# V of each attention unit in one transfer, another order of early loads, and a second score buffer that also takes values

## The chip, the cores and the metric

The kernel runs on one core of a Trainium2 chip. The core has a matrix engine (TensorE: PE in the profile, and PEld for the loading of its stationary operand), VectorE (DVE), ScalarE (ACT), GpSimd (POOL), an engine that mostly issues transfers (SyncE, SP) and 16 DMA engines that they share. The metric is the device time of one execution in microseconds (us). Before the change three runs took 886.68, 889.40 and 889.49 us; the median is 889.40.

## The reference

Three stages follow one another, all in float32:

```python
# B=4, 8 heads, S=576, D=64; q, k, v: (4, 8, 576, 64)
scores = (q @ k.transpose(0, 1, 3, 2)) / 8
# heads 0..3: only the 32 latest positions; heads 4..7: only positions equal mod 32, not later
scores = where(mask, scores, -1e9); scores -= max(scores)
attn = exp(scores); attn /= sum(attn) + 1e-9
x = (attn @ v), heads side by side            # (2304, 512)
x = (sigmoid(x @ w_gate) * (x @ w_val)) @ w_out     # d_ff 1536
h = x @ w_in                                        # d_ff 2048
out = (max(h, 0) + log1p(exp(-abs(h)))) @ w_out2    # (2304, 512)
```

## The kernel before

**Precision.** A float32 matrix product is done as three products of high and low parts (`mm3`, lines 72 to 74). Activations are split on the chip (xh, xl). The weights come as packed 64-bit words in pieces of 128x512 (`raw`, 512 KB, line 109) and are decoded into their two parts by `decode_steps`: VectorE (lines 129, 133, 139, 146), ScalarE (157, the high part) and GpSimd (159 and 160, the low part).

**Attention.** It is cut into 16 units, one per batch and pair of heads; each batch has two local units (0, 1; 4, 5; ...) and two strided ones (2, 3; 6, 7; ...). A unit i passes through:

- `load(i)` and `load_v(i)`: transfers of Q (928), K (929) and V (947). V is stored in two halves of partitions, from 0 and from 64: for a local unit 64 partitions with 10 and 8 chunks of positions, for a strided one 54 partitions each, one transfer per half;
- `bias(i)` (1033) writes the mask into PSUM by a matmul, `scores(i)` (1052) adds QK in 48 or 80 small matmuls; VectorE takes the maximum (1070) and subtracts it (1071);
- `exponent(i)` on ScalarE (1078), `normalize(i)`: sums on VectorE (1085 to 1088), and the multiplication on GpSimd (1091);
- `p_transposes(i)`: six TensorE transposes (1114), copied out of PSUM by ScalarE (1118, later 1120);
- `values(i)` (1131): 72 matmuls for a local unit, 48 for a strided one, into a tile of `ps_o`;
- `outputs(i)`: ScalarE writes xh (1156), VectorE xl (1159).

After these come the gate and value products of the first gated layer, the second layer and the softplus layer; the first matmuls of the gates (lines 72 to 74, tile ps_g) are woven between the later units.

**Order.** Every engine executes its instructions in the order in which the program issues them; a framework adds the semaphore waits that the data and the buffers call for. For units 0 to 4 the order is written out by hand in `first()`; TURN is 4, the first unit of the second batch; from unit 5 on a function `stage(u)` takes over. Transfers of SP are issued in program order too, so a transfer that waits holds all behind it. `hold(t)` (line 100) puts a 1x1 GpSimd memset on a tile ahead of its load: the transfer then waits until GpSimd has come to that point. Eight semaphores (DMAHW0 to DMAHW7) go round among SP's transfers, so each also waits for the one that used its semaphore before.

**Buffers.** V has three buffers, and unit 3's V lies in a part of `acc[1]`; raw weights have three. In PSUM, in use at first are `ps_s` (scores), `ps_o` (values), and two pools that are closed at `early.close()`: `ps_s1` (the scores of units 1 and 3) and `ps_t` (transposes). What these two held is then given to `ps_hy` (three banks, which hold ps_g and its like) and `ps_x` (one bank).

Of the kernel before, what the change touches and what calls it, by code (L numbers as in the profile page):

```python
# [9 lines left out]
F32 = mybir.dt.float32  # L10
# [8 lines left out]
B, H, S, D = 4, 8, 576, 64  # L19
NT, DM = B * S, H * D  # L20
DFF, DFF2 = 1536, 2048
P = 128
STRIDE = 32
NPAIR = H // 2
NLP = NPAIR // 2
# [5 lines left out]
SQ = RG * NJ  # L31
HP = P // 2
HR = 2
NC = S // LQ
SLOTS_L = -(-NC // 4)
NL = (NC + 2) // 2, (NC - 2) // 2
RH = STRIDE // HR
NS = -(-RH // RG)
# [10 lines left out]
def tile_sparse_attention_moe_moe2(  # L49
# [10 lines left out]
    nc = tc.nc  # L60
# [812 lines left out]
    def attention():  # L873
        with ExitStack() as actx:
# [17 lines left out]
                "g": pool("gp", 1), "t": pool("tp", 2), "d": pool("decp", 1), "e": nc.gpsimd,  # L892
            }
            early = ExitStack()
            ps_s1, ps_t = (
                early.enter_context(tc.tile_pool(name=name, bufs=bufs, space=PSUM))
                for name, bufs in (("ps_s1", 1), ("ps_t", 2))
            )

            units = [(b, hp) for b in range(B) for hp in range(NPAIR)]  # L900
# [33 lines left out]
            def load_v(i, held=False):  # L934
                b, hp = units[i]
                loc, w, m, ns = dims(i)
                if i == NPAIR - 1:
                    t = acc[1][:, 0:NL[0] * 2 * D].rearrange("p (n h d) -> p n h d", h=2, d=D)
                else:
                    t = vp.tile([P, NL[0], 2, D], F32, tag="v", name="vt")  # L940
                src = vl[b, hp] if loc else vs[b, hp - NLP]
                if held:
                    hold(t[:, 0, 0, :])
                for r in range(HR):
                    n = NL[r] if loc else NS
                    o = r * HP
                    nc.sync.dma_start(out=t[o:o + w, 0:n], in_=src[r * w:(r + 1) * w, 0:n])
                vt[i] = t

            todo.extend((g, m, c) for g in range(2) for m in range(3) for c in range(GC))  # L950
# [6 lines left out]
            load_v(0)  # L957
            load(3)
            load_v(1)

            scratch = acc[NBA - 1]
            ident = scratch[:, 0:P]
# [160 lines left out]
            def values(i):  # L1123
                loc, w, m, ns = dims(i)
                pt, vv = pts.pop(i), vt.pop(i)
                ps = ps_o.tile([P, 2, TB], F32, tag="o", name="ps_o")
                for r, c, s, p0 in chunks(loc):
                    rows = slice(r * HP, r * HP + w)
                    o = s // 2 * P + p0
                    for h in range(2):  # L1130
                        nc.tensor.matmul(
                            ps[h * D:(h + 1) * D, r, c * m:(c + 1) * m],
                            lhsT=vv[rows, c, h, :], rhs=pt[rows, h, o:o + m],
                            start=True, stop=True,
                        )
                outs[i] = ps
# [51 lines left out]
            def first():  # L1188

                decs = [decode_steps(pools, refill) for refill in (False, False, True)]  # L1190
                swap = lambda: pools.update(f=[other])
                bias(0)
                scores(0)
                masks[False] = table("m_str", P + 2 * LK, SQ, SLOTS_S, strided)
                bias(1)
                scores(1)
                keep_busy(1)
                exponent(0)
                normalize(0)
                load_next(held=True)  # L1200
                load_next()
                bias(2)
                scores(2)
                exponent(1)
                normalize(1)
                load_v(2, held=True)
                load_v(3)
                keep_busy(1)
                bias(3)
                scores(3)  # L1210
                exponent(2)
                p_transposes(0)
                exponent(3)
                normalize(2)
                load(4, held=True)
                normalize(3)
                load_next(held=True)
                values(0)
                outputs(0)
                p_transposes(1)  # L1220
                p_transposes(2)
                next(decs[0])
                next(decs[0])
                load(5, held=True)
                values(1)
                outputs(1)
                p_transposes(3)
                swap()
                next(decs[1])
                next(decs[1])  # L1230
                load_next(held=True)
                load_v(4)
                values(2)
                outputs(2)
                bias(TURN)
                scores(TURN)
                early.close()
                pools["hy"] = pool("ps_hy", 3, space=PSUM)
                pools["x"] = pool("ps_x", 1, space=PSUM)
                values(TURN - 1)  # L1240
                outputs(TURN - 1)
                exponent(TURN)
                normalize(TURN)
                load(6, held=True)
                load_v(5)
                load_next()
                next(decs[2])
                yield
                next(decs[2])
                yield  # L1250
# [199 lines left out]
def _layout(inputs):  # L1450
# [25 lines left out]
        0, 1, 2, 4, 5, 3, 6  # L1476
    )
    z = z.reshape(B, NPAIR - NLP, 2, HR, NS, SQ, D).transpose(0, 1, 3, 5, 4, 2, 6)
    vs = np.ascontiguousarray(z).reshape(B, NPAIR - NLP, HR * SQ, NS, 2, D)

    def w_in(w):
        return w.reshape(NCC, P, -1, GC, P).transpose(2, 1, 3, 0, 4).reshape(-1, P, WE)
# [37 lines left out]
```

## Time and profile before

| what | us |
|---|---|
| median of three runs | 889.40 |
| lowest and highest run | 886.68, 889.49 |
| the profiled execution's own time | 887.71 |
| its span (first to last instruction) | 885.9 |
| PE busy in the span | 864.1 |

The profile is of one execution. Its mean granted TensorE clock is 0.994 of full speed. How the rows of the trace read:

- the page's first line gives, for each engine, busy us, share of the span, and instructions;
- a table of stretches has: start and end in us, length, then for PE, PEld, DVE, ACT and POOL the busy us and in brackets the number of instructions, the granted TensorE clock as a share of full speed, the busy share of the 16 DMA engines, and GB/s;
- a timeline of an engine has: start in us, length of the whole group in us, engine, line, operation, out<-in, shapes, the number of instructions, and in square brackets the idle time ahead of the group and what ended it ("issue": nothing that the profile shows). Matmuls overlap, so a group's length can reach into the next;
- the list of transfers gives: how many, KB of each, and the median us from issue to landing.

### The profile page before, as it was taken

Reading aid. Unit: us, or ns where it says so; the run is one execution under the profiler, and the core shown is the slowest. Engines: PE = TensorE matmul, PEld = TensorE weight load, DVE = VectorE, ACT = ScalarE, POOL = GpSimd, SP = SyncE. Lnnn points to the kernel's source line nnn. Section 1 sums busy time; section 2 is a strip of 40 time slices with the busy share of each in tenths; the row PEclk is TensorE's granted clock in tenths of the full one; section 3 lists DMA queues with packets and bytes.
Section 4 is the critical chain, followed back from the end, with each engine's and each line's share of the span. In section 5 each row is a group of like instructions: output and inputs, shape, how many; then the busy total and the mean of one; then the engine's idle time right before and its main releaser. Section 6 shows DMA issues by size and latency. Waiting matters only on the chain.

```text
span 885.9 us, 15388 instructions
## 1 busy us (share of the span) xinstructions
PE 864.1 (98%) x6008; PEld 725.1 (82%) x6008; DVE 600.3 (68%) x898; ACT 421.3 (48%) x680; POOL 490.7 (55%) x396
## 2 busy tenths in 40 slices
PE   7789999999999999999999999999999999999998
PEld 5668888888888888888888888888888878888887
DVE  5876876268878888878874645665756674656575
ACT  2456544423333333233333466666667575665641
POOL 5563321037888687688778625466536963343530
PEclk9899999999999999999999999999999999999999
DMA  7796450034675567566643245566665565545403
GB/s 245 191 260 165 125 156 9 1 99 139 237 257 195 190 242 243 182 214 225 227 166 158 76 148 176 191 198 197 198 231 187 189 220 184 186 149 181 152 1 118
DMA packets 61367, 153.01 MB, mean 173 GB/s; under 512 B 6160, under 2 KB 6672, under 8 KB 61296
## 3 DMA queue, kind: packets, MB, share of 16 engines
q1 hardware_dynamic: 61008, 151.42, 53.6%
q8 instruction: 47, 0.77, 0.4%
q10 hardware_dynamic: 288, 0.62, 0.2%
q14 instruction: 24, 0.20, 0.1%
HBM read 113.75 MB, written 38.27 MB: 172 GB/s over the span
## 4 chain that ended last, share of the span: by engine, by line
PE 72%; DVE 3%; ACT 1%; POOL 1%; issue 1%; DMA 0%; DVEq 0%; POOLq 0%; ACTq 0%; SPq 0%
PE ps_y L72 10%; PE ps_y L73 10%; PE ps_y L74 10%; PE ps_v L74 4%; PE ps_v L72 4%; PE ps_v L73 4%; PE ps_h L73 4%; PE ps_h L74 4%; PE ps_h L72 4%; PE ps_g L72 4%; PE ps_g L74 4%; PE ps_g L73 4%; PE ps_b L72 2%; PE ps_b L73 2%; PE ps_b L74 2%
## 5 line engine op out<-in xcount | busy, mean ns | idle before, releaser
L335 POOL TENSOR_TENSOR b<-b,b 128x512 f32<-128x512 f32 (+1 forms) x42 | 72.4, 1738 | 91.7 <-DVE gl L335 46.1
L248 ACT ACTIVATE gh<-ps_v 128x512 fp32r<-128x512 f32 (+1 forms) x60 | 33.3, 555 | 131.1 <-DVE ps_v L289 131.0
L309 DVE TENSOR_TENSOR acc<-ps_y,acc 128x512 f32<-128x512 f32 (+1 forms) x100 | 62.1, 633 | 48.0 <-PE ps_y L74 47.6
L338 ACT ACTIVATE gh<-b 128x1024 fp32r<-128x1024 f32 (+1 forms) x63 | 57.8, 917 | 40.6 <-DVE b L718 22.7
L474 DVE TENSOR_TENSOR acc<-ps_y,acc 128x512 f32<-128x512 f32 x66 | 44.8, 686 | 39.5 <-PE ps_y L74 38.4
L335 POOL TENSOR_TENSOR gl<-b,gh 128x1024 fp32r<-128x1024 f32 x20 | 49.1, 2457 | 36.5 <-ACT gh L338 36.5
L249 DVE TENSOR_TENSOR gl<-ps_v,gh 128x512 fp32r<-128x512 f32 (+1 forms) x60 | 38.3, 638 | 37.5 <-ACT gh L248 37.5
L196 POOL TENSOR_TENSOR a<-f,e 128x512 f32<-128x512 f32 x32 | 41.4, 1293 | 39.5 <-DVE e L146 39.5
L184 POOL TENSOR_TENSOR pair<-a,pair 128x512 fp32r<-128x512 f32 x32 | 41.5, 1296 | 31.9 <-ACT pair L183 31.9
L335 DVE TENSOR_TENSOR gl<-b,gh 128x1024 fp32r<-128x1024 f32 (+1 forms) x43 | 48.8, 1137 | 14.4 <-ACT gh L338 14.3
L72 PE MATMUL ps_y<-gh,w12h 128*128 128x512 f32 (+1 forms) x144 | 54.0, 375 | 0.1
L74 PE MATMUL ps_y<-gh,w02l 128*128 128x512 f32 (+1 forms) x144 | 53.7, 373 | 0.0
L73 PE MATMUL ps_y<-gl,w12h 128*128 128x512 f32 (+1 forms) x144 | 53.6, 373 | 0.0
L289 DVE TENSOR_TENSOR ps_v<-ps_v,sg 128x512 f32<-128x512 f32 (+1 forms) x60 | 38.5, 641 | 21.2 <-PE ps_v L74 20.0
L74 PE MATMUL ps_y<-gh,w12l 128*128 128x512 f32 (+1 forms) x140 | 52.2, 373 | 0.2 <-POOL w12l L160 0.2
L72 PE MATMUL ps_y<-gh,w02h 128*128 128x512 f32 (+1 forms) x136 | 51.3, 377 | 0.7 <-ACT acc L307 0.6
L183 ACT ACTIVATE pair<-s 128x512 fp32r<-128x512 f32 x32 | 20.2, 632 | 66.4 <-POOL s L210 51.8
L133 DVE SCALAR_TENSOR_TENSOR f<-raw,ps_x 128x512 uint32<-128x512 uint32 x66 | 45.4, 688 | 8.9 <-POOL w11l L160 2.1
L73 PE MATMUL ps_y<-gl,w02h 128*128 128x512 f32 (+1 forms) x136 | 50.6, 372 | 0.0
L146 DVE SCALAR_TENSOR_TENSOR e<-raw,ps_x 128x512 f32<-128x512 uint32 x66 | 45.3, 687 | 2.3
L139 DVE TENSOR_SCALAR ps_x<-f 128x512 uint32<-128x512 uint32 x66 | 45.4, 688 | 0.9
L72 PE MATMUL ps_g<-xh,w00h 128*128 128x512 f32 (+1 forms) x120 | 45.5, 379 | 0.0
(359 smaller groups left out, 2809.0 us busy)
## 6 DMA issues: line engine op xcount, KB each, us to landing
raw<-in_w_dram SPq DMA_DIRECT2D x68, 512.0 KB, 4.6
in_s<-pair SPq DMA_DIRECT2D x32, 512.0 KB, 3.4
out_s<-pair SPq DMA_DIRECT2D x32, 512.0 KB, 2.9
xh<-in_s SPq DMA_DIRECT2D x64, 256.0 KB, 3.3
xl<-in_s SPq DMA_DIRECT2D x56, 256.0 KB, 3.2
out_dram<-acc SPq DMA_DIRECT2D x16, 256.0 KB, 2.0
w10h<-out_s SPq DMA_DIRECT2D x6, 512.0 KB, 5.8
w10l<-out_s SPq DMA_DIRECT2D x6, 512.0 KB, 4.0
```

The source lines that it names most:

```text
L72: nc.tensor.matmul(ps, lhsT=lh, rhs=rh, start=first, stop=False, **kw)
L73: nc.tensor.matmul(ps, lhsT=lh, rhs=rl, start=False, stop=False, **kw)
L74: nc.tensor.matmul(ps, lhsT=ll, rhs=rh, start=False, stop=last, **kw)
L133: nc.vector.scalar_tensor_tensor(out=f, in0=high, scalar=0xC0000000, in1=part, op0=ALU.bitwise_and, op1=ALU.bitwise_or,)
L139: nc.vector.tensor_scalar(out=e, in0=f, scalar1=0xFF800000, scalar2=None, op0=ALU.bitwise_and)
L146: nc.vector.scalar_tensor_tensor(out=e.bitcast(F32), in0=low, scalar=2.0 ** -52, in1=x.bitcast(F32), op0=ALU.mult, op1=ALU.mult,)
L184: nc.gpsimd.tensor_tensor(out=l, in0=src, in1=h.bitcast(F32), op=ALU.subtract)
L196: nc.gpsimd.tensor_tensor(out=a, in0=f.bitcast(F32), in1=e.bitcast(F32), op=ALU.add)
L309: nc.vector.tensor_tensor(out=y, in0=ps[:, 0:n], in1=y, op=ALU.add)
L335: eng.tensor_tensor(out=out, in0=a, in1=b, op=ALU.subtract)
L338: nc.scalar.activation(out=op[0], in_=src, func=AF.Copy)
L474: nc.vector.tensor_tensor(out=y, in0=ps, in1=y, op=ALU.add)
```

## The change

Three things change. V comes to each unit in one transfer of 128 partitions: for the strided units the host pads the halves to 64 rows with zeros, and for the local ones the second half is loaded with all 10 chunks, of which `values` reads 8 as before. Second, the loads in `first()` are released in another order: two raw loads come ahead of the V of unit 2, unit 4's Q and K come earlier, unit 4's V waits for a memset behind the first decode, and the second step of decode 1 follows the outputs of unit 2. Third, values(1) and values(3) write to the pool `ps_s1` instead of `ps_o`; the order of the two closed pools is swapped, and values(3) and outputs(3) come ahead of `early.close()`.

```diff
--- before.py
+++ after.py
@@ -892,9 +892,9 @@
                 "g": pool("gp", 1), "t": pool("tp", 2), "d": pool("decp", 1), "e": nc.gpsimd,
             }
             early = ExitStack()
-            ps_s1, ps_t = (
+            ps_t, ps_s1 = (
                 early.enter_context(tc.tile_pool(name=name, bufs=bufs, space=PSUM))
-                for name, bufs in (("ps_s1", 1), ("ps_t", 2))
+                for name, bufs in (("ps_t", 2), ("ps_s1", 1))
             )
 
             units = [(b, hp) for b in range(B) for hp in range(NPAIR)]
@@ -938,13 +938,10 @@
                     t = acc[1][:, 0:NL[0] * 2 * D].rearrange("p (n h d) -> p n h d", h=2, d=D)
                 else:
                     t = vp.tile([P, NL[0], 2, D], F32, tag="v", name="vt")
-                src = vl[b, hp] if loc else vs[b, hp - NLP]
                 if held:
                     hold(t[:, 0, 0, :])
-                for r in range(HR):
-                    n = NL[r] if loc else NS
-                    o = r * HP
-                    nc.sync.dma_start(out=t[o:o + w, 0:n], in_=src[r * w:(r + 1) * w, 0:n])
+                n = NL[0] if loc else NS
+                nc.sync.dma_start(out=t[:, 0:n], in_=vl[b, hp] if loc else vs[b, hp - NLP])
                 vt[i] = t
 
             todo.extend((g, m, c) for g in range(2) for m in range(3) for c in range(GC))
@@ -957,6 +954,7 @@
             load_v(0)
             load(3)
             load_v(1)
+            load_next()
 
             scratch = acc[NBA - 1]
             ident = scratch[:, 0:P]
@@ -1123,7 +1121,10 @@
             def values(i):
                 loc, w, m, ns = dims(i)
                 pt, vv = pts.pop(i), vt.pop(i)
-                ps = ps_o.tile([P, 2, TB], F32, tag="o", name="ps_o")
+                if i < TURN and i % 2:
+                    ps = ps_s1.tile([P, 2, TB], F32, tag="s", name="ps_o")
+                else:
+                    ps = ps_o.tile([P, 2, TB], F32, tag="o", name="ps_o")
                 for r, c, s, p0 in chunks(loc):
                     rows = slice(r * HP, r * HP + w)
                     o = s // 2 * P + p0
@@ -1198,13 +1199,13 @@
                 exponent(0)
                 normalize(0)
                 load_next(held=True)
-                load_next()
+                load_v(2)
                 bias(2)
                 scores(2)
                 exponent(1)
                 normalize(1)
-                load_v(2, held=True)
-                load_v(3)
+                load_v(3, held=True)
+                load(4)
                 keep_busy(1)
                 bias(3)
                 scores(3)
@@ -1212,37 +1213,36 @@
                 p_transposes(0)
                 exponent(3)
                 normalize(2)
-                load(4, held=True)
+                load_next(held=True)
                 normalize(3)
-                load_next(held=True)
+                load(5, held=True)
                 values(0)
                 outputs(0)
                 p_transposes(1)
                 p_transposes(2)
                 next(decs[0])
                 next(decs[0])
-                load(5, held=True)
+                load_v(4, held=True)
+                load_next()
                 values(1)
                 outputs(1)
                 p_transposes(3)
                 swap()
                 next(decs[1])
-                next(decs[1])
-                load_next(held=True)
-                load_v(4)
                 values(2)
                 outputs(2)
+                next(decs[1])
+                load(6, held=True)
                 bias(TURN)
                 scores(TURN)
+                values(TURN - 1)
+                outputs(TURN - 1)
                 early.close()
                 pools["hy"] = pool("ps_hy", 3, space=PSUM)
                 pools["x"] = pool("ps_x", 1, space=PSUM)
-                values(TURN - 1)
-                outputs(TURN - 1)
                 exponent(TURN)
                 normalize(TURN)
-                load(6, held=True)
-                load_v(5)
+                load_v(5, held=True)
                 load_next()
                 next(decs[2])
                 yield
@@ -1476,7 +1476,9 @@
         0, 1, 2, 4, 5, 3, 6
     )
     z = z.reshape(B, NPAIR - NLP, 2, HR, NS, SQ, D).transpose(0, 1, 3, 5, 4, 2, 6)
-    vs = np.ascontiguousarray(z).reshape(B, NPAIR - NLP, HR * SQ, NS, 2, D)
+    vs = np.zeros((B, NPAIR - NLP, HR, HP, NS, 2, D), f)
+    vs[:, :, :, :SQ] = z
+    vs = vs.reshape(B, NPAIR - NLP, P, NS, 2, D)
 
     def w_in(w):
         return w.reshape(NCC, P, -1, GC, P).transpose(2, 1, 3, 0, 4).reshape(-1, P, WE)
```

**SyncE, the first transfers behind Q and K of units 0 to 2.** vt is unit 0's, then unit 1's, then unit 2's V; acc_64 is unit 3's V; the Q and K in between are unit 3's. Before:

```order
L947 DMA vt<-in_vl_dram 64x1280
L947 DMA vt<-in_vl_dram 64x1024
L928 DMA qt<-in_q_dram 128x622
L929 DMA kt<-in_k_dram 128x612
L947 DMA vt<-in_vl_dram 64x1280
L947 DMA vt<-in_vl_dram 64x1024
L109 DMA raw<-in_w_dram 128x512 x2
L947 DMA vt<-in_vs_dram 54x768 x2
L947 DMA acc_64<-in_vs_dram 54x768 x2
```

After:

```order
L944 DMA vt<-in_vl_dram 128x1280
L928 DMA qt<-in_q_dram 128x622
L929 DMA kt<-in_k_dram 128x612
L944 DMA vt<-in_vl_dram 128x1280
L109 DMA raw<-in_w_dram 128x512 x2
L944 DMA vt<-in_vs_dram 128x768
L944 DMA acc_64<-in_vs_dram 128x768
```

Each V has become one instruction; both raw loads still stand ahead of the V of unit 2.

**SyncE, the transfers behind Q and K of unit 4.** The raw loads are weights of decodes 2 and 3, Q and K are unit 5's, and vt is unit 4's V. Before, then after:

```order
L109 DMA raw<-in_w_dram 128x512 [waits DMAHW4_49,Pool_49]
L928 DMA qt<-in_q_dram 128x576 [waits DMAHW5_49,Pool_49]
L929 DMA kt<-in_k_dram 128x608 [waits DMAHW6_49]
L109 DMA raw<-in_w_dram 128x512 [waits DMAHW7_49,DVE_49,Pool_49]
L947 DMA vt<-in_vl_dram 64x1280 [waits DMAHW0_49,PE_49]
L947 DMA vt<-in_vl_dram 64x1024 [waits DMAHW1_49]
```

```order
L109 DMA raw<-in_w_dram 128x512 [waits DMAHW0_49,Pool_49]
L928 DMA qt<-in_q_dram 128x576 [waits DMAHW1_49,Pool_49]
L929 DMA kt<-in_k_dram 128x608 [waits DMAHW2_49]
L944 DMA vt<-in_vl_dram 128x1280 [waits DMAHW3_49,Pool_49]
L109 DMA raw<-in_w_dram 128x512 [waits DMAHW4_49,DVE_49]
```

Unit 4's V stood behind a raw load that waits for GpSimd and VectorE, and itself waited for PE; now it waits for GpSimd's memset and stands ahead of that raw load.

**TensorE, from values(2) to the first gates matmul (ps_g).** Between them stand bias(4), scores(4) and values(3), whose operands lie in acc_64. Before:

```order
L1131 MATMUL ps_o<-pt,vt 64x54 [waits DMAHW6_49,DVE_49,PE_49]
L1131 MATMUL ps_o<-pt,vt 64x54
L1131 MATMUL ps_o<-pt,vt 64x54 [waits DMAHW7_49]
L1131 MATMUL ps_o<-pt,vt 64x54 x21
L1033 MATMUL ps_s<-m_loc,one 128x320 x2
L1052 MATMUL ps_s<-kt,qt 32x64 [waits DMAHW3_49,DMAHW2_49]
L1052 MATMUL ps_s<-kt,qt 32x64 x39
L1131 MATMUL ps_o<-acc_64 64x54 [waits DMAHW0_49,DVE_49]
L1131 MATMUL ps_o<-acc_64 64x54 [waits Activation_49]
L1131 MATMUL ps_o<-acc_64 64x54 [waits DMAHW1_49]
L1131 MATMUL ps_o<-acc_64 64x54 x21
L72 MATMUL ps_g<-xh,w00h 128x512
L73 MATMUL ps_g<-xl,w00h 128x512
```

After:

```order
L1132 MATMUL ps_o<-pt,vt 64x54 [waits DMAHW4_49,DVE_49]
L1132 MATMUL ps_o<-pt,vt 64x54 x23
L1031 MATMUL ps_s<-m_loc,one 128x320 x2
L1050 MATMUL ps_s<-kt,qt 32x64 [waits DMAHW7_49,DMAHW6_49]
L1050 MATMUL ps_s<-kt,qt 32x64 x39
L1132 MATMUL ps_o<-acc_64 64x54 [waits DMAHW5_49,DVE_49,Activation_49]
L1132 MATMUL ps_o<-acc_64 64x54 [waits Activation_49]
L1132 MATMUL ps_o<-acc_64 64x54 x22
L72 MATMUL ps_g<-xh,w00h 128x512 [waits DVE_49]
L73 MATMUL ps_g<-xl,w00h 128x512
```

The first matmul of values(2) has lost a wait for PE, each V one semaphore, and the first gates matmul has a wait for VectorE that it did not have; by the program, that wait is for xl of outputs(3).

**VectorE, from xl of unit 1 to xl of unit 3.** acc_63 holds the working words of decode 1; ps_s are unit 4's scores; the rows with 128x2x18x16 are xl of units 2 and 3. Before:

```order
L1159 TENSOR_TENSOR xl<-ps_o,xh 128x320 [waits PE_49,Activation_49]
L1159 TENSOR_TENSOR xl<-ps_o,xh 128x256
L129 TENSOR_SCALAR acc_63<-raw 128x512 [waits DMAHW5_49]
L133 SCALAR_TENSOR_TENSOR acc_63<-raw,acc_63 128x512 [waits DVE_49]
L139 TENSOR_SCALAR acc_63<-acc_63 128x512 [waits DVE_49]
L146 SCALAR_TENSOR_TENSOR acc_63<-raw,acc_63 128x512 [waits DVE_49]
L1159 TENSOR_TENSOR xl<-ps_o,xh 128x2x18x16 [waits Activation_49]
L1070 TENSOR_REDUCE st<-ps_s 128x2x5 [waits PE_49]
L1071 TENSOR_TENSOR sl_109<-ps_s,st 128x640 [waits DVE_49]
L1159 TENSOR_TENSOR xl<-ps_o,xh 128x2x18x16 [waits Activation_49]
```

After:

```order
L1160 TENSOR_TENSOR xl<-ps_o,xh 128x320 [waits PE_49,Activation_49]
L1160 TENSOR_TENSOR xl<-ps_o,xh 128x256
L129 TENSOR_SCALAR acc_63<-raw 128x512 [waits DMAHW3_49]
L133 SCALAR_TENSOR_TENSOR acc_63<-raw,acc_63 128x512 [waits DVE_49]
L1160 TENSOR_TENSOR xl<-ps_o,xh 128x2x18x16 [waits Activation_49]
L139 TENSOR_SCALAR acc_63<-acc_63 128x512 [waits DVE_49]
L146 SCALAR_TENSOR_TENSOR acc_63<-raw,acc_63 128x512 [waits DVE_49,Pool_49]
L1068 TENSOR_REDUCE st<-ps_s 128x2x5 [waits PE_49]
L1069 TENSOR_TENSOR sl_109<-ps_s,st 128x640 [waits DVE_49]
L1160 TENSOR_TENSOR xl<-ps_o,xh 128x2x18x16 [waits Activation_49]
```

Unit 2's xl now stands between the two halves of decode 1; xl of unit 3 is still the last of the ten.

## Rows read from the trace of the kernel before

**Rows 1.** the page: busy us, share, instructions of each engine

```profile
PE 864.1 (98%) x6008; PEld 725.1 (82%) x6008; DVE 600.3 (68%) x898; ACT 421.3 (48%) x680; POOL 490.7 (55%) x396
```

**Rows 2.** table of stretches, the opening and 400 us of the steady part

```profile
0.00:50.00 50.00, 37.74 (x861) 29.49 (x861) 33.70 (x64) 17.21 (x32) 26.52 (x54) 0.90 0.79 225
100.00:500.00 400.00, 398.81 (x2525) 335.34 (x2524) 296.18 (x466) 140.26 (x243) 258.77 (x230) 1.00 0.50 168
```

**Rows 3.** timeline of PE from 12 to 66 us

```profile
15.01 1.54 PE L1052 MATMUL ps_s<-kt,qt 64*64 64x54 f32 x48 [2.15 <-DMA kt<-in_k_dram]
...
21.26 0.30 PE L1131 MATMUL ps_o<-pt,vt 64*64 64x32 f32 x3 [1.47 <-issue]
...
27.72 0.92 PE L1131 MATMUL ps_o<-pt,vt 54*64 54x54 f32 x48 [0.91 <-PE ps_p L1114]
...
31.33 0.93 PE L1131 MATMUL ps_o<-acc 54*64 54x54 f32 x48 [1.24 <-DVE xl L1159]
32.19 0.50 PE L72 MATMUL ps_g<-xh,w00h 128*128 128x512 f32 x1
...
35.96 0.44 PE L1114 MATMUL ps_p<-one,sl 128*128 128x128 f32 x2 [0.86 <-POOL sl L1091]
...
39.91 0.31 PE L1131 MATMUL ps_o<-pt,vt 64*64 64x32 f32 x4 [1.24 <-DMA vt<-in_vl_dram]
41.01 1.39 PE L1131 MATMUL ps_o<-pt,vt 64*64 64x32 f32 x68 [0.79 <-DMA vt<-in_vl_dram]
...
54.33 0.76 PE L1052 MATMUL ps_s<-kt,qt 64*64 64x54 f32 x35 [0.38 <-DMA kt<-in_k_dram]
...
63.69 0.54 PE L1052 MATMUL ps_s<-kt,qt 64*32 64x64 f32 x34 [1.89 <-issue]
```

**Rows 4.** table of stretches by the shape of the transfers in flight

```profile
3.00:6.80 3.80, 3.42 (x58) 2.18 (x58) 0.40 (x2) 0.00 (x0) 3.12 (x14) 1.00 1.05 402
7.50:10.00 2.50, 2.50 (x84) 2.00 (x84) 2.34 (x5) 0.71 (x1) 0.00 (x0) 1.00 1.00 220
19.00:22.00 3.00, 1.53 (x57) 1.39 (x50) 1.21 (x4) 0.54 (x3) 2.54 (x5) 0.92 0.57 179
```

**Rows 5.** timeline of SP's queue

```profile
7.95 0.43 SPq L929 DMA_DIRECT2D kt<-in_k_dram  x1
...
17.66 0.68 SPq L947 DMA_DIRECT2D acc<-in_vs_dram  x2
...
33.43 1.11 SPq L947 DMA_DIRECT2D vt<-in_vl_dram  x2
```

**Rows 6.** table of stretches, two at half clock

```profile
15.00:18.00 3.00, 2.99 (x55) 2.57 (x55) 1.66 (x4) 0.44 (x1) 1.43 (x3) 0.50 0.84 273
42.00:45.00 3.00, 3.00 (x22) 2.41 (x15) 1.29 (x3) 1.83 (x5) 2.00 (x3) 0.50 1.01 226
```

**Rows 7.** timeline of POOL from 10 to 50 us

```profile
12.78 1.40 POOL L1091 TENSOR_TENSOR sl<-sl,st 128x320 f32<-128x320 f32 x2 [5.55 <-DVE st L1088]
...
27.00 1.27 POOL L160 TENSOR_TENSOR w00l<-f,e 128x512 fp32r<-128x512 f32 x1
...
32.89 0.09 POOL L100 MEMSET raw<- 1x1 f32 x1
```

**Rows 8.** timeline of ACT, the exponent of unit 2

```profile
14.19 0.74 ACT L1078 ACTIVATE ss<-ss 128x648 f32<-128x648 f32 x1 [2.00 <-DVE ss L1071]
```

**Rows 9.** timeline of DVE, first and last of ten instructions

```profile
26.79 0.82 DVE L1159 TENSOR_TENSOR xl<-ps_o,xh 128x320 fp32r<-128x320 f32 x2 [1.31 <-ACT xh L1156]
...
33.00 0.76 DVE L1159 TENSOR_TENSOR xl<-ps_o,xh 128x576 fp32r<-128x576 f32 x1
```

**Rows 10.** table of stretches, the ten instructions on DVE

```profile
26.79:33.76 6.97, 4.83 (x186) 4.11 (x186) 6.65 (x11) 3.29 (x6) 4.59 (x6) 1.00 0.29 90
```

**Rows 11.** transfers of the first 70 us, local V

```profile
vt<-in_vl_dram SPq DMA_DIRECT2D x6, 256.0 KB, 8.7
```

**Rows 12.** the page: PE's instruction queue, packets and MB

```profile
q8 instruction: 47, 0.77, 0.4%
```

## The prediction

> **What bounds the kernel now.** I read the page first: PE is busy 864.1 us, 98% of the span [rows 1]. Then the table of stretches: from 100 to 500 us PE is busy 398.81 of 400 us, in the first 50 only 37.74 [rows 2]. So some 12 of PE's 22 idle us lie in the stretch the change rearranges, and what PE gains there stays: later the other engines wait for PE. Third, PE's own timeline with the idle time ahead of each group and what ended it [rows 3]. The stops are: 2.15 us at 15.01 for the K of unit 3, 1.47 at 21.26 for nothing the profile shows, 0.91 at 27.72 ahead of values(2), 1.24 at 31.33 ahead of values(3) for VectorE's xl, 0.86 for POOL at 35.96, 1.24 and 0.79 for unit 4's V at 39.91 and 41.01, 0.38 for a K at 54.33. Last the clock: PE runs at 0.50 of full speed, 1.2 GHz, from 15 to 18 and from 42 to 45 us, each time after such stops [rows 6]; 3 us at half speed cost 1.5 us of full-speed work.
>
> I follow one number: the start of the first gates matmul, 32.19 us before [rows 3]. Ahead of it lie only unit work and stops.
>
> **Part 1, V in one transfer.** At 3.0 to 6.8 us 128-partition transfers move 402 GB/s, at 7.5 to 10, with the two 64-partition V transfers of unit 0 in flight, 220 [rows 4]. The K of unit 3 is issued at 7.95, right behind [rows 5], and is waited for until 15.01. Unit 0's V is now 128x1280 fp32, 655 KB instead of 590: at 402 GB/s 1.6 us instead of 2.7 at 220. Q and K of unit 3, 632 KB, take another 1.6, so that K lands near 11 us. PE is free for it from 12.86 (15.01 less 2.15): the whole 2.15 goes. Bounds: nothing gained (rival A) to 2.15; I take 2.15, because the row at 402 is the same kind of transfer on the same queue 3 us earlier. For the strided V, 54 partitions at 179 GB/s with 0.57 of the engines' time in use [rows 4] become 128 (padded, 393 KB instead of 332). Those of units 2 and 3 were issued until 17.66 plus 0.68 [rows 5]; now they go out near 15 and 17, behind POOL's memsets (one stands behind 14.18, one 2.7 us later). Even at 8.7 us to landing, the most that the other V took [rows 11], they are there at 23.7 and 25.7, ahead of values(2) and values(3) below, by 0.3 and 0.7 us. I cost them at zero; without that cover it is what they come late.
>
> The Trainium skill speaks against this part: DMA: Bandwidth & Descriptors, section "Why a DMA increments its semaphore by 16 and not by 1", lets a transfer use the largest number of engines up to 16 that divides its slowest dimension, 16 for 64 partitions as for 128; by it alone merging local V buys nothing, and the sum would be rival A's. The row agrees on the engines (share 1.00) and not on the rate (220 against 402). SBUF — State Buffer, "Door 1: The DMA port swizzle", explains that: 64 partitions reach only half of the ports, and by it the sum is my own.
>
> With K early, scores(3) run 12.86 to 13.8 (48 matmuls of this width take 0.92 at full clock at 27.72, 1.54 here [rows 3]). p_transposes(0) need POOL's normalising, done at 14.18 [rows 7], and end at 15.0. The ACT copies of pt stand behind the exponent of unit 2, 14.19 to 14.93 [rows 8]; then values(0) start at 15.7 and end their first 69 matmuls at 17.0. I keep the 1.47 stop, so PE goes on at 18.5 where it was 21.26: 2.75 us ahead (2.15, and 0.6 for the clock). The two transposes behind stay at half speed as before. values(1), 24.45 before, begin at 21.7.
>
> **Part 2, the second score buffer.** values(2) no longer wait for outputs(1), values(3) no longer for outputs(2): 0.91 and 1.24 us go [rows 3]. values(3) ended at 32.2; now 32.2 - 2.75 - 0.91 - 1.24 = 27.3. That would be 4.9 us of gain.
>
> But a wait is added. The gates' first accumulator lies in a bank that values(3) now use, so the first gates matmul waits for xl of outputs(3), the last of a fixed row of ten instructions on VectorE, from xl(1) to xl(3). Before, they ran from 26.79 to 33.76 (33.00 plus 0.76): 6.97 us [rows 9], with VectorE busy 6.65 of them [rows 10]. xl(1) needs values(1) and an ACT copy; it moves with values(1), by 2.75, to 24.04. So xl(3) ends near 31.0, and the gates start there: 1.2 us ahead of 32.19, not 4.9. The other 3.7 us are PE idle. Behind this wait stands all of PE's queue: gates, bias(5), scores(5). Bounds of the new wait: 3.4 us if the ten run with no gap (6.65), 4.9 if all of the lead goes. I take 3.7, since the order of the ten has hardly changed. After a stop of that size, the two half-speed stretches tell me to expect another: +1.5 [rows 6].
>
> **Part 3, the order of releases.** Unit 4's V was issued at 33.43, behind a raw load that POOL released at 32.89 and that also waited for VectorE [rows 5, 7]. Now only a memset behind the first decode's L160 releases it; that ended at 28.27 (27.00 plus 1.27) [rows 7] and moves with the 2.75, to 25.5. The ordinary local V took 8.7 us from issue to landing [rows 11]; so it lands by 34.2. PE asks for it near 38.1 (39.91, less 1.24 of stop, less 1.2, plus 1.5, less the 0.86 below). The two stops, 2.03 us, go, and the half-speed stretch after them, 1.5. Bounds: nothing, if it lands as late behind PE's demand as now; 3.5 at most.
>
> POOL's normalising of unit 4 hangs on VectorE's sums right behind xl(3): about 31.0 plus 1.1, and 1.4 on POOL, done at 33.5. PE reaches those transposes after six gates matmuls, bias and scores(5), at half speed some 4.5 us after 31.0: 35.5. The 0.86 goes (bounds: 0 to 0.86). The K load waited for at 54.33 is released earlier, too: 0.38 goes.
>
> Instruction fetch: 0.77 MB in 47 packets [rows 12] are 16 KB each; with 6008 matmuls and as many weight loads [rows 1] that is 256 instructions a packet, and the stops with no releaser fall 256 instructions apart. Of eight such borders up to 65 us five show a stop, the largest 1.47 at 21.26 and 1.89 at 63.69 [rows 3], some 4.5 in all, and three none, at places where PE stood still for something else. One of these may come to light: between 0 and 1.89; as the other three share 1.1 us, I take +0.5.
>
> **The sum**, against the profiled execution's own 887.71: -1.2 +1.5 -2.03 -1.5 -0.86 -0.38 +0.5 = -4.0, so 883.7. That execution lies 1.7 below the median of the three runs (889.40; 886.68 to 889.49); between 883.7 and 885.4 from the median I take 884.2.
>
> **The rivals.**
> A, the merged V is no faster: K of unit 3 still ends PE's wait at 15.01. For it: the 64-partition transfers already show share 1.00, and 65 KB are added. Against it: 402 GB/s. Then values(3) end at 30.05, xl(3) still at 33.76, and the gates start 1.6 late instead of 1.2 early: +1.6 +1.5 -2.03 -1.5 -0.86 -0.38 +0.5 = -1.2, that is 2.8 above the forecast, 887.0. No change, by measure.
>
> B, slower: PE's instruction stream becomes the bound of the opening. The stops that PE now has give its fetch time to catch up; without them each of the eight borders may cost as much as the dearest, 1.89 [rows 3]: 15.1 us instead of 4.5, +10.6 on top of the sum: 894.8. It decides once the fetches cost 7 us more than now. For it: three borders that cost nothing now lie in stops that go. Against: from 100 to 500 us, at PE busy without stops, 1.2 us are idle over some 20 borders [rows 2]. The Trainium skill, Runtime: NRT & Kernel Launch, "Instruction fetch mechanics", calls such a border mostly hidden; in this opening the trace differs.
>
> C, the new wait takes everything: the clock stays at half through the gates and into values(4), another 1.5, and the ten VectorE instructions take all of the lead, another 1.2: -4.0 + 2.7 = -1.3, 886.9: no change. For it: a stop of 2.15 and one of 2.03 each brought 3 us at half speed [rows 3, 6], and this one is longer. Against: those rows show 3 us, and no more.
>
> D, better: no half-speed stretch after the new wait (1.5), no border added (0.5): -6.0, 882.2; and if the 1.47 of stop at 21.26 goes as well, with K early, 880.7.
>
> **How the numbers follow.** The forecast 0.60, A 0.14, C 0.08, B 0.08, D 0.10. A difference under 0.3%, 2.7 us, cannot be told from none here. Faster: the forecast but for its upper tail, and D: 0.69. Same: A, C and that tail: 0.22. Slower: B and a little: 0.09. The forecast's own range is 882 to 886.5; D extends it down to 880.5, A, C and the scatter of the runs up to 888.5. B is left out.
>
> **What would show it.** Right: no wait for a K at scores(3), which start before 13.5 us; no stop ahead of values(2) and values(3); values(3) end near 27.3; then one stop of 3 to 4 us ahead of the first gates matmul, ended by VectorE's L1160; unit 4's V issued by 26 us and no wait for it. Wrong: gates starting later than 32.2 (A), stops with no releaser adding up to over 8 us in the first 65 (B), or a granted clock at half beyond 36 us (C).

## The result and the profile after

The changed kernel takes 880.15 us in the median of six runs (877.92 to 881.29); the kernel before, in six runs, 887.10 (886.29 to 889.49). The ratio of the means is 0.9915 with a 95% interval of 0.9895 to 0.9934: some 7 us faster. The profiled execution took 881.29 (span 879.5), against 887.71 (885.9) before: 6.4 less. The forecast was 884.2, and the low end of its range 880.5; the direction was right, the size too small.

The page, which answers to [rows 1]:

```profile
PE 861.7 (98%) x6008; PEld 722.3 (82%) x6008; DVE 601.2 (68%) x898; ACT 420.7 (48%) x680; POOL 491.8 (56%) x396
```

PE's timeline, which answers to [rows 3] (same columns):

```profile
12.21 0.92 PE L1050 MATMUL ps_s<-kt,qt 64*64 64x54 f32 x48 [0.67 <-DMA kt<-in_k_dram]
...
16.55 0.30 PE L1132 MATMUL ps_o<-pt,vt 64*64 64x32 f32 x3 [0.44 <-issue]
...
21.33 0.69 PE L1132 MATMUL ps_o<-pt,vt 54*64 54x54 f32 x32
24.26 0.45 PE L1132 MATMUL ps_o<-pt,vt 54*64 54x54 f32 x16 [2.24 <-issue]
...
28.19 0.89 PE L1132 MATMUL ps_o<-acc 54*64 54x54 f32 x19 [0.94 <-issue]
30.61 0.79 PE L72 MATMUL ps_g<-xh,w00h 128*128 128x512 f32 x1 [1.53 <-DVE xl L1160]
...
35.34 1.28 PE L1112 MATMUL ps_p<-one,sl 128*128 128x128 f32 x6
...
37.95 1.35 PE L1132 MATMUL ps_o<-pt,vt 64*64 64x32 f32 x72
...
43.88 0.44 PE L1112 MATMUL ps_p<-one,sl 128*128 128x128 f32 x2 [0.58 <-issue]
...
57.19 0.48 PE L72 MATMUL ps_y<-gh,w02h 128*128 128x512 f32 x1
...
58.57 0.49 PE L73 MATMUL ps_y<-gl,w02h 128*128 128x512 f32 x1 [0.21 <-DVE gl L249]
59.49 0.50 PE L74 MATMUL ps_y<-gh,w02l 128*128 128x512 f32 x1 [0.42 <-POOL w02l L160]
```

Unit 3's K is waited for 0.67 us and its scores start at 12.21. values(2), at 21.33, wait for nothing and then stand still for 2.24 in their midst, values(3) for 0.94; the first gates matmul waits 1.53 for xl and starts at 30.61. After that the stops of before for POOL, for V and for the K loads are gone, up to the first ps_y, the output products at 57.19. In the trace before, those begin here:

```profile
64.79 0.48 PE L72 MATMUL ps_y<-gh,w02h 128*128 128x512 f32 x1
```

The stops without a releaser ("issue") from 5 to 65 us come to as much as before, 4.46 against 4.49, but at other places: 3.88 of them lie ahead of the gates (1.70 before) and 0.58 behind (2.79).

So the gain, step by step through the profiled executions: 2.8 us at scores(3), 1.6 at the gates, 7.6 at the output products, 6.4 at the end; 0.63 of what is given back are the two waits at 58.57 and 59.49.

The transfers, 7 to 9 us, with unit 0's V in flight (before, then after; a table of stretches as [rows 4]):

```profile
7.00:9.00 2.00, 2.00 (x92) 1.50 (x78) 1.39 (x2) 0.00 (x0) 0.23 (x1) 1.00 1.06 239
```

```profile
7.00:9.00 2.00, 1.79 (x83) 1.19 (x83) 1.97 (x5) 0.34 (x1) 0.24 (x1) 1.00 1.01 402
```

All 16 engines are busy in both; one moves 239 GB/s and the other 402.

The clock, which answers to [rows 6], and what VectorE, ScalarE and SP did (their own timelines, as [rows 9], [rows 8] and [rows 5]):

```profile
26.00:30.00 4.00, 2.13 (x62) 1.65 (x49) 3.01 (x6) 0.89 (x2) 3.07 (x3) 0.50 0.73 280
30.00:36.00 6.00, 5.39 (x91) 4.31 (x92) 4.86 (x9) 1.02 (x2) 3.36 (x5) 0.50 0.59 179
```

```profile
28.12 0.83 DVE L1069 TENSOR_TENSOR sl<-ps_s,st 128x640 f32<-128x640 f32 x1
29.80 0.76 DVE L1160 TENSOR_TENSOR xl<-ps_o,xh 128x576 fp32r<-128x576 f32 x1 [0.85 <-ACT xh L1157]
```

```profile
29.11 0.65 ACT L1157 ACTIVATE xh<-ps_o 128x576 fp32r<-128x576 f32 x1 [3.17 <-PE ps_o L1132]
```

```profile
24.62 0.33 SPq L944 DMA_DIRECT2D vt<-in_vl_dram  x1
```

VectorE was idle for 0.85 us ahead of xl of unit 3, waiting for xh, and ScalarE for 3.17 ahead of that xh, waiting for PE. So the added wait is one unit's way through ScalarE and VectorE after values(3), not the row of ten instructions. The half speed begins at 26.0, in values(3) and 4.6 us ahead of the first gates matmul, and lasts until 36.3. Unit 4's V was issued at 24.62, and PE did not wait for it.

### The profile page after: what moved, and what is told of

The parts are those of the page before. It is cut to its first block, busy times and chain, and to the rows that moved or that the text cites. A ratio compares the mean times of both kernels' runs of the same rounds, so it can differ in the third digit from the quotient of the medians.

```text
span 879.5 us, 15371 instructions
## 1 busy us (share of the span) xinstructions
PE 861.7 (98%) x6008; PEld 722.3 (82%) x6008; DVE 601.2 (68%) x898; ACT 420.7 (48%) x680; POOL 491.8 (56%) x396
## 4 chain that ended last, share of the span: by engine, by line
PE 72%; DVE 3%; ACT 2%; POOL 1%; issue 1%; DVEq 0%; POOLq 0%; ACTq 0%
PE ps_y L72 10%; PE ps_y L73 10%; PE ps_y L74 10%; PE ps_v L74 4%; PE ps_v L72 4%; PE ps_v L73 4%; PE ps_h L73 4%; PE ps_h L74 4%; PE ps_h L72 4%; PE ps_g L74 4%; PE ps_g L72 4%; PE ps_g L73 4%; PE ps_b L72 2%; PE ps_b L73 2%; PE ps_b L74 2%
## 5 line engine op out<-in xcount | busy, mean ns | idle before, releaser
L196 POOL TENSOR_TENSOR a<-f,e 128x512 f32<-128x512 f32 x32 | 41.5, 1297 | 39.6 <-DVE e L146 39.6
```

The source lines that it names most:

```text
L196: nc.gpsimd.tensor_tensor(out=a, in0=f.bitcast(F32), in1=e.bitcast(F32), op=ALU.add)
```

## The experiments

All times are medians. Ratios, in brackets their intervals, are of the means of the runs, against the kernel before on the same chip.

**What each part is worth.** First V alone, in the kernel before (the host's padding of the strided V goes with it):

```diff
-                for r in range(HR):
-                    n = NL[r] if loc else NS
-                    o = r * HP
-                    nc.sync.dma_start(out=t[o:o + w, 0:n], in_=src[r * w:(r + 1) * w, 0:n])
+                n = NL[0] if loc else NS
+                nc.sync.dma_start(out=t[:, 0:n], in_=vl[b, hp] if loc else vs[b, hp - NLP])
```

> The kernel before with V merged into one transfer, and nothing else. Theory F (the instruction fetch of TensorE waits behind V transfers of 64 partitions, which keep all 16 DMA engines busy at half the rate): K of unit 3 is there in time (2.15 us and about 0.6 of clock), and the stops without a releaser after 45 us (0.54, 0.36 and 1.89 us before) fall to under 1 us in all; 4 to 6 us faster than before, 881 to 883. Theory K (merging helps unit 3's K alone, and the late stops that vanished are scatter): those late stops stay near 2.8 us; 2 to 3.5 us faster, 883.5 to 885. Theory O (the order of releases did it): within 1 us of before, 886 to 888.

Measured: 882.54, ratio 0.9936 (0.9912 to 0.9960). And the reverse, the changed kernel with the removed lines back, the host's layout of V included:

> The changed kernel with V in two transfers again, as before; order of releases and second score buffer stay. F: the wait for unit 3's K is back (about 2 us), and late stops without a releaser too (2 us or more after 40 us); 4 to 6 us slower than the changed kernel, 884 to 886. K: 2 to 3.5 us slower, late stops as in the changed kernel (0.6 us). O: within 1 us of the changed kernel, 879 to 881.

Measured: 888.39, ratio 1.0004 (0.9984 to 1.0025). So without the merge the other two parts together give nothing that can be told from none; the merge is worth 5 us in the old order and 8 in the new one. Theory O is out. The fetch stops after 45 us were 0.71 us in the first, as F had it and not K, and 0.84 in the second, not the 2 that F asked for; and the second lost more than either.

**The second score buffer.** All values back in ps_o:

```diff
-                if i < TURN and i % 2:
-                    ps = ps_s1.tile([P, 2, TB], F32, tag="s", name="ps_o")
-                else:
-                    ps = ps_o.tile([P, 2, TB], F32, tag="o", name="ps_o")
+                ps = ps_o.tile([P, 2, TB], F32, tag="o", name="ps_o")
```

> The changed kernel with all values in ps_o as before; merged V and order of releases stay. Then values(2) wait for xl of unit 1, values(3) for xl of unit 2, and the first gates matmul waits for no xl. If the second buffer is worth the two waits that it removes (0.91 and 1.24 us): 2 us slower than the changed kernel, 882. If, as the trace of the changed kernel suggests, it only trades them for the wait on xl of unit 3 (1.53 us, and the clock behind it): values(2) start about 1.6 later, inside what was a stop for instructions, the gates start at 29 to 30 instead of 30.6, and the time is 879 to 880.5.

Measured: 877.22, ratio 0.9892 (0.9872 to 0.9912): faster than either forecast. With only values(1) in the second buffer (`if i == 1:`):

> The changed kernel with only values(1) in the second score buffer, values(3) in ps_o: the first gates matmul no longer waits for xl of unit 3, values(3) wait for xl of unit 2, which ended at 26.2, where values(3) started anyway. If the wait on xl is a real cost: gates start at 29.1 instead of 30.6, with no half clock from 30.6 to 35 or a shorter one; 1.5 to 3 us faster than the changed kernel, 877 to 878.7. If it is hidden anyway (the next wait, for POOL's normalising of unit 4, takes its place): 879.7 to 880.5.

Measured: 878.25, ratio 0.9893 (0.9876 to 0.9911). The gates start at 28.15 there, without a wait: it is values(3) in the second buffer that costs. The changed kernel and the one with one buffer again, on one chip:

> The changed kernel unchanged, beside the run with one buffer on the same chip. The first gates matmul waits 1.53 us for xl of unit 3 again, and the stretch behind it is at half clock again for some 5 us; time 879.5 to 881. If the first profile of it was untypical: another wait, or none.

> All values in ps_o, merged V, new order of releases, again, beside the changed kernel. If the second buffer really costs: 2.5 to 3.5 us faster than the changed kernel, 876.5 to 878. If the first difference was between chips: within 1 us of it.

Measured: 880.38 (0.9916 to 0.9940) for the changed kernel and 877.90 (0.9887 to 0.9915) with one buffer. The second buffer costs 2.5 to 2.9 us. PE's timeline with one buffer, the first run:

```profile
22.96 0.96 PE L1129 MATMUL ps_o<-pt,vt 54*64 54x54 f32 x48 [1.67 <-issue]
...
25.74 0.67 PE L1129 MATMUL ps_o<-acc 54*64 54x54 f32 x29 [0.36 <-DVE xl L1157]
27.68 0.55 PE L1129 MATMUL ps_o<-acc 54*64 54x54 f32 x19 [1.26 <-issue]
28.16 0.50 PE L72 MATMUL ps_g<-xh,w00h 128*128 128x512 f32 x1
```

VectorE's xl of unit 1 in the same run:

```profile
22.04 0.82 DVE L1157 TENSOR_TENSOR xl<-ps_o,xh 128x320 fp32r<-128x320 f32 x2
```

values(2) start 1.67 us late. The profile names no releaser, but xl of unit 1 ended at 22.86, 0.1 ahead of them, and with V alone merged the same stop of 1.67 is put down to that xl: I read it as the old wait, come back. They no longer stop in their midst, where two buffers had 2.24. values(3) wait 0.36 for VectorE and stop for 1.26 in their midst; the gates start at 28.16 with no wait, 2.45 us ahead of the changed kernel. The granted clock from 12 to 36 us in the second run with one buffer, and in the second run of the changed kernel:

```profile
12.00:36.00 24.00, 18.43 (x569) 14.65 (x570) 22.93 (x38) 11.30 (x23) 15.85 (x23) 1.00 0.79 257
```

```profile
12.00:36.00 24.00, 18.68 (x494) 14.98 (x494) 22.90 (x39) 10.66 (x22) 15.81 (x23) 0.86 0.77 264
```

In the first runs it is 0.93 and 0.79 on this stretch, with only values(1) in the second buffer 1.00.

Order of releases and merge, without the buffer, are the version that beats both kernels; against V alone (882.54) the order is worth 5 us.

**Where the merge pays.** Two transfers again for some units only, in the changed kernel:

```diff
+                src = vl[b, hp] if loc else vs[b, hp - NLP]
+                if i < NPAIR:
+                    nc.sync.dma_start(out=t[:, 0:n], in_=src)
+                else:
+                    for r in range(HR):
+                        n = NL[r] if loc else NS
+                        o = r * HP
+                        nc.sync.dma_start(out=t[o:o + w, 0:n], in_=src[o:o + w, 0:n])
```

Units 4 to 15 in two, as shown (for the others the condition is `i >= NPAIR`, `i not in (0, 1)` and `i not in (2, 3)`):

> The changed kernel with V in two transfers again for units 4 to 15 alone; units 0 to 3 keep one. Theory F (instruction fetch waits behind 64-partition V transfers wherever they fall): stops without a releaser after 40 us rise from 0.6 us to 2 or more; 2 to 3 us slower than the changed kernel, 882 to 883. Theory E (what merging buys, it buys by 35 us, through unit 3's K and the stops among units 0 to 3; the late stops are scatter): late stops 1 us or less, 879.5 to 881.

Units 0 to 3 in two:

> The changed kernel with V in two transfers again for units 0 to 3 alone. E: everything of the merge is lost, as in the run without any merge: K of unit 3 waited for about 2.2 us, stops without a releaser of 4 us or more from 20 to 34 us, gates from 34 to 35; 885 to 889. F: only half is lost, 882 to 884.

Units 0 and 1, and units 2 and 3:

> The changed kernel with only units 0 and 1 (local) loading V in two 64-partition transfers; all others keep one. With units 0 to 3 split, 7 us were lost. Theory L (the local V ahead of unit 3's K hold up that K and the instruction fetches near 10 to 20 us): all or most of it, 885 to 888, K waited for about 2.2 us. Theory S (the 54-partition V of units 2 and 3 hold up the fetches from 20 to 30 us): only the K wait, 882 to 883.5.

> The changed kernel with only units 2 and 3 (strided) loading V in two 54-partition transfers. L, and the prediction, which put these V at zero: 879.5 to 881. S: 883 or more, with stops without a releaser of 4 us or more from 20 to 34 us (3.2 in the changed kernel).

Measured: 882.16 (0.9925 to 0.9958) for units 4 to 15, 887.11 (0.9973 to 1.0011) for 0 to 3, 887.28 (0.9979 to 1.0011) for 0 and 1, 880.86 (0.9935 to 0.9972) for 2 and 3. So the local V of the first two units carries some 7 us by the median. Its twelve runs fall into two groups, five from 882.9 to 884.3 and seven from 887.1 to 888.8, so what a run loses is about 3 or about 8. The strided V ahead of values(2) costs 0.5 us by the median, against 880.38 for the changed kernel on the same chip, and the prediction had it at zero; but three of its eight runs took 884.5 to 885.4, which none of the changed kernel's eleven did, so it is not shown to cost nothing. The later V carries 2, against 879.98 for V in two wide transfers (below) on the same chip. E and L hold for the early part; F's forecast for the late part came in, too. PE's timeline with units 4 to 15 in two:

```profile
45.47 0.44 PE L1119 MATMUL ps_p<-one,sl 128*128 128x128 f32 x2 [2.87 <-issue]
...
52.46 0.44 PE L1057 MATMUL ps_s<-kt,qt 64*64 64x54 f32 x12 [0.59 <-issue]
```

The stop of 0.58 us at this place has become 2.87. The profile shows instruction packets among the transfers (queue, packets, MB, share of the engines' time in the stretch); the one that ends this stop, and its counterpart in the changed kernel:

```profile
q8 instruction: 1, 0.02, 7.9%
```

```profile
q8 instruction: 1, 0.02, 6.2%
```

```profile
42.00:45.40 3.40, 0.60 (x6) 0.36 (x4) 2.95 (x4) 0.00 (x0) 3.03 (x4) 1.00 0.99 240
```

```profile
41.00:43.00 2.00, 2.00 (x56) 1.67 (x55) 0.26 (x2) 0.19 (x1) 1.89 (x3) 1.00 1.02 353
```

The packet starts at 42.9 in the one and at 41.5 in the other, lasts 1.27 and 1.00 us, and PE goes on some 2.6 and 2.3 after its start. Until it starts, PE has run out: its last matmul before the stop ended at 42.6. Around it, 64-partition V keeps the 16 engines busy 0.99 at 240 GB/s; in the other, they are as busy (1.02), at 353. In the sixteen profiles, each of the 59 stops without a releaser from 5 to 65 us ended 1.9 to 3.9 us after the start of an instruction packet, 56 of them 2.2 to 3.1; but for the two of 1.67 with one buffer, I read these stops as the fetch. That V of 64 partitions is what holds it up is not shown by these rows: in the second run of the changed kernel, with wide V, the same place has a stop of 1.33. Over all profiles the stops of this kind from 40 to 65 us come to 0.31 to 3.46 us in the five with later V in two transfers of 64 partitions or fewer, and to 0 to 1.33 in the eleven with wide ones: more with narrow V, but the two overlap. What I did not try is a change to the fetch itself.

**Width or number of transfers.** Each V in two transfers of all 128 partitions:

```diff
-                nc.sync.dma_start(out=t[:, 0:n], in_=vl[b, hp] if loc else vs[b, hp - NLP])
+                src = vl[b, hp] if loc else vs[b, hp - NLP]
+                for c in (slice(0, n // 2), slice(n // 2, n)):
+                    nc.sync.dma_start(out=t[:, c], in_=src[:, c])
```

> The changed kernel with each V in two transfers of 128 partitions, half of the chunks each: the same bytes, the partitions of the change, the number of transfers of before. Theory W (the width in partitions sets the rate, 400 against 230 GB/s): as the changed kernel, 879 to 881, K of unit 3 waited for 1.1 us or less. Theory N (the number of transfers matters: one more issue of 0.4 to 0.5 us and one more of the eight semaphores for each V): 883 to 887, K waited for 1.5 us or more.

Measured: 879.98, ratio 0.9920 (0.9903 to 0.9937). W: the width decides, the number of transfers does not. scores(3) wait for no K at all, but they also come later in this execution (bias(3), their line 1033, at 12.08, in the changed kernel 11.08):

```profile
12.08 0.46 PE L1033 MATMUL ps_s<-m_str,one 128*128 128x324 f32 x2
12.47 0.92 PE L1052 MATMUL ps_s<-kt,qt 64*64 64x54 f32 x48
```

**The scatter, and the clock.** The kernel before, profiled again:

> The kernel before, unchanged, for a second profile. In the first, the matmuls of units 0 to 2 ran at half speed from 5 to 12 us, and in the changed kernel at full speed. If that was scatter of one execution: full speed here too, and the wait for unit 3's K about 0.7 longer (2.8 us), with scores(3) starting at 15.0 all the same. If it belongs to the kernel: half speed again. Stops without a releaser beyond 45 us: 2 us or more again if they belong to the kernel, under 1 if they were scatter.

Measured: 886.50. The 80 matmuls of scores(0) took 1.04 us, as in the changed kernel, K was waited for 1.67 us and the fetch ahead of it took 1.87; scores(3) started at 15.28; the late fetch stops were 0.31. So these stops, and where the clock is low, differ between executions of one kernel. In the run with units 0 and 1 in two transfers, whose profiled execution was the slowest of twelve (882.92 to 888.80), from 16 to 44 us:

```profile
16.00:44.00 28.00, 23.06 (x469) 19.11 (x461) 17.52 (x31) 9.47 (x19) 13.37 (x20) 0.51 0.59 200
```

Some 27 us at half clock. Does the stop for K cost by its length, or by this? Eight more dummy matmuls ahead of unit 3's scores put work into the stop and load nothing earlier:

```diff
-                keep_busy(1)
+                keep_busy(9)
                 bias(3)
                 scores(3)
```

In that run, and in the kernel before:

> The run with only units 0 and 1 loading V in two transfers, with the same eight more dummy matmuls ahead of unit 3's bias and scores. Its profile without them was at half clock from 16 to 44 us, and its median 887.3. C: clock 1.00 from 12 to 24 us, 3 to 5 us faster, 882.5 to 884.5. D: 886.5 to 888.5.

> The kernel before with eight more dummy matmuls of 512 columns (0.23 us each at full clock, 1.8 us in all) ahead of unit 3's bias and scores, where TensorE waits 1.7 to 2.2 us for unit 3's K; nothing is loaded earlier. Theory C (most of what the late K costs is the clock: after that stop TensorE runs at half speed for 3 to some 25 us): granted clock 1.00 from 12 to 20 us in place of 0.55 to 0.83, and 2 to 4 us faster than before, 883 to 885. Theory D (only the delay itself counts): the dummies replace idle time by work, within 1 us of before, 886 to 888.

Measured: 882.59 (ratio 0.9933, 0.9906 to 0.9959) where it was 887.28 (0.9995): the time is what C forecast, 4.7 us less. In the kernel before, 886.77 (0.9986, 0.9966 to 1.0007): no gain that can be told from none, as D had it. Their profiles:

```profile
16.00:44.00 28.00, 24.86 (x575) 20.49 (x574) 22.14 (x38) 12.01 (x26) 14.27 (x21) 0.70 0.73 246
```

```profile
15.25 0.92 PE L1052 MATMUL ps_s<-kt,qt 64*64 64x54 f32 x48 [0.55 <-DMA kt<-in_k_dram]
...
21.34 0.65 PE L1131 MATMUL ps_o<-pt,vt 64*64 64x32 f32 x11 [2.72 <-issue]
...
31.70 1.01 PE L1131 MATMUL ps_o<-acc 54*64 54x54 f32 x48 [1.43 <-DVE xl L1159]
```

The first has a granted clock of 0.70 on the same stretch, not 0.51; full speed throughout, as C had it, it is not. Its scores(3) start later, too (16.26 against 15.48), and a stop of 2.27 without a releaser ahead of the gates is gone. None of its six runs, 882.0 to 884.5, falls where the slower group was. So it is shown that work in the stop pays there, and not that it does so by the clock alone. In the second scores(3) and values(0) run at full speed, and then PE stops for 2.72 us for the fetch, which costs what was won.

## Why the prediction was right in direction and too small

**The bound, right.** PE was the bound, and all of the difference arises in the first 65 us (7.6 us at the output products, of which 1.2 are lost again later).

**K of unit 3, right, but a little late.** At 402 GB/s as said; it was still waited for, for 0.67 us, and scores(3) started at 12.21 instead of 12.86 only because the units before had run faster: the 80 matmuls of scores(0) took 1.04 us, and 1.41 in the profile before. The granted clock reads 1.00 from 5 to 12 us in both, so there it does not show the difference. 128 partitions in one transfer or in two give the same time, 64 partitions do not. With that the trace agrees with the Trainium skill, SBUF — State Buffer, "Door 1: The DMA port swizzle": 64 partitions reach half of the ports. By the rule on the number of engines that the prediction cites nothing would have changed; 402 against 239 GB/s at the same share says otherwise.

**values(2) and values(3), right on the waits, wrong on what was behind.** Neither waits for an xl any more. But values(3) ended at 29.08, not 27.3: two fetch stops, 2.24 and 0.94, came to light there.

**The new wait: the start right (30.61 against 31.0), but by luck.** I had the row of ten instructions on VectorE as the limit, 3.7 us of stop behind values(3) that end at 27.3. Measured were 1.53 behind values(3) that end 1.8 later, the way of one tile through ScalarE and VectorE: two errors that cancel. The half speed of 3 us that I put behind this wait was there for nearly 6 us, but it had begun 4.6 us ahead of the gates, after the stop of 2.24; in the second run of the changed kernel it ends at 28 and comes back at 31. So what of it this wait brings stays open. And I never compared with the kernel without the second buffer. My own terms make the buffer a loss of some 3 us (3.7 of stop and 1.5 of clock against 0.91 and 1.24 gained), a sum that I did not draw; without it the gates start 2.45 us earlier, and it costs 2.5 to 2.9.

**Unit 4's V, POOL and the later K, right.** No wait is left for any: 2.03, 1.10 and 0.66 us (0.86 and 0.38 were in the sum). PE came to values(4) at 37.95, forecast 38.1. The strided V at zero: right by the median, with the three slower runs above against it.

**The step that failed: the instruction fetch, +0.5.** Behind the gates the stops without a releaser were 0.54, 0.36 and 1.89 before and are 0.58 after: -2.2, not +0.5. These 2.7 us, with 0.24 of POOL and 0.28 of K that I had left out, are what the interval from the gates to the output products gained beyond the sum (6.0 against 2.8); 1.2 of it are given back by the end. Ahead of the gates the same stops grew from 1.70 to 3.88, but there they only made values(3) later and the wait for xl shorter, by about as much. I had the fetch as a matter of how fast PE eats its instructions, with one more border that comes to light where another stop goes. In its place the runs show stops that move and differ between executions, and that are longer where the later V goes over 64 partitions, which costs 2 us for units 4 to 15; that the transfers of V hold up the packets is argued from that, and the cause stays open. The Trainium skill, Runtime: NRT & Kernel Launch, "Instruction fetch mechanics", calls the cost of such a border mostly hidden; here single ones cost up to 2.87 us. Since these stops differ between executions, the profiled pair shows one case. Of the 4.05 us between the forecast and the median 2.4 are the sum, 0.5 the step from it to the forecast, and 1.1 that the profiled execution was the slowest of six.

**The term beside it: the clock.** I priced the late K at 2.15 and 0.6 of clock. Splitting V for units 0 and 1 costs 7 us in the changed kernel, of which 4.7 come back when the stop is filled with work, part of it in fetch stops. A stop does not cost 1.5 us of clock each time: from nothing to 27 us at half speed were seen. Why the half speed lasts so differently stays open, and so does why the filling does nothing for the kernel before, but for the one fetch stop that its profile shows.

**The rivals.** A was wrong, by the rate. B, the fetch as a bound, was wrong in size: the stops without a releaser stayed at 4.5 us, not over 8, though those ahead of the gates did grow. C had the longer half speed right (to 36.3 us) and the rest not. D's time, 880.7 to 882.2, came nearest, and its border behind the gates was indeed not added; its full clock came only without values(3) in the second buffer, in two profiles of three.

## What to carry to other kernels

A load over 64 partitions can keep every DMA engine busy at little more than half the rate (239 against 402 GB/s here); look for what it costs in what is loaded behind it, as unit 3's K here, and look at the instruction packets, too. Price a stop of the matrix engine by the clock behind it and by its scatter over executions, not by its length alone. Where a change swaps one wait for another, work out the variant without the swap too: here it is the faster one.

## What the hardware showed that I had not expected

Instruction fetches for TensorE take 0.9 to 1.6 us per 16 KB packet (six of 151 in the first 66 us longer, up to 2.4), and TensorE goes on mostly 2.2 to 3.1 us after the packet starts. In stretches of small matmuls that shows: by the 0.92 us for 48 matmuls, 256 instructions (128 matmuls and their loads) last an estimated 2.5 us. The same program had stops without a releaser of 4.5 us up to 65 us in one execution and of 2.2 in another. Eight dummy matmuls in a stop made one kernel 4.7 us faster, though they add 1.8 us of work, and another not measurably.
